# Inverse-transform steps ahead of spectra, and four attention scores in a row behind the last maxima, in a long convolution beside attention

## The chip, the cores and the metric

The kernel runs on one core of a Trainium2 chip. TensorE (PE) does the matmuls, VectorE (DVE), ScalarE (ACT) and GpSimd (POOL) the elementwise work, and nearly all transfers are issued from the queue of SyncE (SP). Each of these executes its own instruction stream in order, and the streams meet at semaphores. The metric is the device time of one launch in microseconds (us); the time before is the median of three runs.

## The reference

Two independent halves are computed from one sequence of 2048 rows and written side by side into one output of 2 x 448 columns.

```python
def _A_ref(u, log_A_real, A_imag, C_real, C_imag, log_dt, D_skip):
    dt = jnp.exp(log_dt)
    A = -jnp.exp(log_A_real) + 1j * A_imag
    C = (C_real + 1j * C_imag) * dt[:, None]
    P = jnp.exp((A * dt[:, None])[:, :, None] * pos[None, None, :])
    K = 2.0 * jnp.einsum("dn,dnl->dl", C, P).real        # D=448, N=256, L=2048
    Kf = jnp.fft.rfft(K, 2 * L)
    Uf = jnp.fft.rfft(u_t, 2 * L)
    y = jnp.fft.irfft(Uf * Kf[None], 2 * L)[:, :, :L]
    return y.transpose(0, 2, 1) + u * D_skip

def _B_ref(x, wqkv, wo):                                 # S=2048, D=448, H=16, Dh=28
    q, k, v = ...                                        # x @ wqkv, by head
    p = softmax(einsum("bhqd,bhkd->bhqk", q, k) * Dh ** -0.5)
    o = einsum("bhqk,bhkd->bhqd", p, v)
    return o.transpose(0, 2, 1, 3).reshape(B, S, D) @ wo
```

The first half is a convolution as long as the sequence, done with a transform, a product of spectra and an inverse transform. The second half is softmax attention without a mask, with 16 heads of width 28.

## The kernel before

A first stage projects x to queries, keys and values and prepares tables for the convolution's kernel. The second stage, the main loop (L1073 on), is the larger part. It has 256 steps, numbered s here. A step is one key tile of 128 keys (kt, 0 to 15) for one unit u; a unit is four heads (a group) and 512 queries, so 16 units make 4 groups by 4 query chunks. In each step TensorE computes four scores of 128 keys by 512 queries (`s0` to `s3`, tiles `pss`, function `s_mm`), ScalarE takes their exponentials (tiles `p`), and TensorE multiplies the exponentials of the step before with the values (`pv`, tile `po`; four matmuls that each use 32 columns of the array). The maxima of the softmax are computed 19 steps ahead by a second set of score matmuls (`m0` to `m3`, tiles `pm`, read by VectorE and ScalarE). With s = 237 the last maxima are done, and the remaining 19 steps, 237 to 255, have no `m`.

The convolution and the output projection are fed into the same loop through slots. One call of `slot` does at most one task. A step has two slots, A ahead of `pv` and B behind it, and from s = 238 a third, C, at the step's end (`FX`). The order of a step is the tuple `ORDER`: m0 s0 m1 s1, slot A, pv, slot B, m2 s2 m3 s3. Everything is emitted in program order, and the engines keep that order. The tasks that a slot can take in the last part are these:

- A **spectrum** (16 of them, 8 for each half of the channels; function `spectrum`): two forward tasks (`yk` with `mw`, 16 matmuls of 32 columns each in the profile's rows), whose results VectorE multiplies with the transformed input (`pr`), then four joins on GpSimd (`p`, function `join`), then two inverse tasks `back` (`p` with `mw`), which ScalarE evicts (`y`) and SP writes to DRAM (`z`). Between the second forward task and the first `back` lie at least GAP = 3 slots. The first two joins give the first `back` its operand, the last two the second.
- A **finish** (8 of them, 4 for each half; function `finish`), the last inverse step: its load brings `zi` from `z` and the input rows `ut`; GpSimd multiplies `ut` with D_skip (the skip); then four tasks of 8 matmuls each (`zi` with `wb`) are added to the skip by VectorE (`ot`) and written out, two at a time. A half's finishes can only be loaded when its eight spectra are done, since `zi` reads what they wrote. The first task of a finish comes three steps after its load at the earliest, and the load of the next one is issued when the first task of this one is placed.
- A **projection** of the attention output (four per query chunk in the last group; 32 matmuls `ua` with `og` and `on`), due when a unit is finished and its divisions by the softmax sums are done on VectorE (`divide`: `rb`, `r`, `pm`, then `on` or `og`). `load_og` loads the three earlier groups' outputs of that chunk at kt = 9 and places their divisions 3, 6 and 9 slots later, each with its second part two slots behind.

When nothing more urgent is due, a slot tries a spectrum first and then a finish, `f_slot(s_, "s") or f_slot(s_, "f")`. Behind the last step the same function empties what is left, two slots to a unit of s.

PSUM has eight banks. In the last part three of them hold `pss`, one `po`, and four are a ring from which all other matmul results are taken in turn (`w_tile`, names `pm`): a task has to wait until the result that was put into its bank four takings earlier has been read.

Of the kernel before, what the change touches and what calls it, by code (L numbers as in the profile page):

```python
# [8 lines left out]
F32 = mybir.dt.float32  # L9
# [13 lines left out]
G = 4  # L23
HG = H // G
CQ = 512
NQ = L // CQ
NK = L // 128
# [5 lines left out]
NS = NU * NK  # L33
LEAD = 3
ORDER = ('m0', 's0', 'm1', 's1', 'v', 'f', 'pv', 'f', 'v', 'k', 'm2', 's2', 'm3', 's3', 'v')
PB = 8
F1 = 2
FX, PD, GAP = 1, 2, 3
# [54 lines left out]
def body(ctx, tc, a, out):  # L93
# [5 lines left out]
    def pool(stack, name, bufs=1, space=None, side=None):  # L99
        kw = {} if space is None else {"space": space}  # L100
        if side:
            kw["side"] = side
        return stack.enter_context(tc.tile_pool(name=name, bufs=bufs, reuse_waits="tile", **kw))
# [23 lines left out]
    def w_tile():  # L127

        n_ring[0] += 1
        return ps_w[0].tile([128, CQ], F32, name=f"pm{n_ring[0] % ps_w[1]}")  # L130
# [25 lines left out]
    def load_v(g, c):  # L156
        v_g[g, c] = t = v_p.tile([128, NK // NQ, HG, 32], F32, name="v", bufs=5)
        nc.sync.dma_start(t.rearrange("p t h e -> p t (h e)"), v_d[c][:, g])

    def load_kd(g, j, rows=range(4)):  # L160
        if 0 in rows:
            kd_g[g, j] = kd_p.tile([128, CQ], F32R, name=f"kdif{j}")
        t = kd_g[g, j]
        for r in rows:
            nc.sync.dma_start(t[r::4].bitcast(F32), kd_d[g][r % 2, 32 * j:32 * j + 32, :])
# [62 lines left out]
    with ExitStack() as st:  # L228
# [368 lines left out]
        for i in range(16):  # L597
            for kc in range(4):
                f, kw = (max_mm, (0, i, kc)) if kc < 2 else (max_pair, (i, kc))
# [13 lines left out]
    ps_s = pool(att, "ps_s", 3, PSUM)  # L613
# [153 lines left out]
            wo_t.append(t)  # L767

    def s_mm(u, kt, j):
        pss = ps_s.tile([128, CQ], F32, name="pss")  # L770
        nc.tensor.matmul(pss, kt_g[u // NQ][j][:, kt * 128:(kt + 1) * 128], q_u[u][:, j, :], start=True, stop=True)
        p = kq_p.tile([128, CQ], F32, name="p", bufs=PB)
        nc.scalar.activation(p, pss, AF.Exp, scale=SCALE)
        return p
# [10 lines left out]
    def divide(o, y, at, then=lambda: None):  # L785

        t_ = {}

        def sums():
            t = kq_p.tile([128, NK, 32], F32, name="rb")  # L790
            nc.vector.transpose(t.rearrange("p b e -> p (b e)"), o)
            t_["r"] = kq_p.tile([128, NK], F32, name="r", bufs=2)
            nc.vector.reciprocal(t_["r"], t[:, :, DH])

        def scale():
            pw = w_tile()
            nc.vector.transpose(pw.rearrange("p (b e) -> p b e", e=32), t_["r"][:, :, None].to_broadcast([128, NK, 32]))
            nc.vector.tensor_tensor(y, o, pw, ALU.mult)
            then()
        later(at, sums)  # L800
        later(at + 2, scale)

    def load_og(u):
        og_u[u] = og = kq_p.tile([128, G - 1, CQ], F32, name="og")
        for g in range(G - 1):
            nc.sync.dma_start(og[:, g], on_d[u % NQ][g])
            divide(og[:, g], og[:, g], n_slot[0] + 3 + 3 * g, lambda: ready.append(u))

    def fin(u, s_):
        g, c = divmod(u, NQ)  # L810
# [122 lines left out]
    urgent, free, ready = collections.deque(), [], []  # L933

    def later(at, f):
        free.append((at, f))
        free.sort(key=lambda t: t[0])
# [9 lines left out]
    def u_part(i, c):  # L947
        u_jobs[i][1 + c]()
        if c and i not in (14, 15):
            u_load(i + 2)  # L950
        if c and i == 15:
            u_load(16)
            u_load(17)
        if c and i == 31:
            load_wo()
# [12 lines left out]
    n_slot, f_next = [0], {"s": 0, "f": 0}  # L968
# [6 lines left out]
    def f_load(s_, kind):  # L975

        if not f_jobs[kind] or f_loaded[kind]:
            return
        _, f, i = f_jobs[kind][0]
        if kind == "f" and s_done[0] < (f + 1) * N1 // 4:  # L980
            return
        if (kind, f, i) == ("f", 0, 0):
            if f_ready["s", 1] == NS:
                return
            f_p["f", 0] = f_p["f", 1] = pool(f1_st, "ff_p")
        if (kind, f) not in f_p or f_ready.get((kind, f), 0) > s_ + 2:
            return
        load, tasks, ahead = job(f_jobs[kind].popleft(), f_p[kind, f], kq_p, w_tile)
        load()
        if ahead:  # L990
            f_ahead.append((s_ + FL[kind] - 1, ahead))
        f_loaded[kind].append((max(f_ready.get((kind, f), 0), s_ + FL[kind]), tasks))

    def f_slot(s_, kind):
        f_load(s_, kind)
        if k_due or powers["e"] or powers["g"]:
            return False
        while f_ahead and f_ahead[0][0] <= s_:
            f_ahead.popleft()[1]()
        if not f_tasks[kind]:  # L1000
            if not f_loaded[kind] or f_loaded[kind][0][0] > s_:
                return False
            f_tasks[kind].extend(f_loaded[kind].popleft()[1])
            f_load(s_, kind)
        gap, t = f_tasks[kind][0]
        if n_slot[0] < f_next[kind] + gap:
            return False
        f_tasks[kind].popleft()
        t()
        s_done[0] += kind == "s" and not f_tasks[kind]  # L1010
        f_next[kind] = n_slot[0]
        f_load(s_, kind)
        return True
# [10 lines left out]
    def slot(s_):  # L1024
        n_slot[0] += 1
        while free and free[0][0] <= n_slot[0]:
            free.pop(0)[1]()
        if urgent and urgent[0][0] <= n_slot[0]:
            urgent.popleft()[2]()
        elif s_ >= NS and f_slot(s_, "s"):  # L1030
            pass
        elif p_due and p_due[0][0] <= s_:
            p_due.popleft()[1]()
        elif m_due and m_due[0][0] <= s_:
            m_due.popleft()[1]()
        elif u_due and u_due[0][0] <= s_:
            u_part(*u_due.popleft()[1:])
        else:
            f_slot(s_, "s") or f_slot(s_, "f")

    def k_seed(s_):
        b = k_due[0] if k_due else NB
# [32 lines left out]
    for s in range(NS):  # L1075
        u, kt = divmod(s, NK)
        sm = s + NK + LEAD
        if s == 12 * NK:
            k0_st.close()
            f_p["s", 0] = f_p["s", 1] = pool(f0_st, "f0_p", side="right")  # L1080
            f_ready["s", 0], f_ready["s", 1] = s, NS
        if s >= 12 * NK and f_ready["s", 1] == NS and not (k_due or m_due or powers["g"] or powers["e"]):
            g_st.close()
            ps_st.close()
            ps_w[:] = pool(ps_st, "ps_f", 4, PSUM), 1
            f_ready["s", 1] = s + F1
        if kt == 9 and u // NQ == G - 1:
            load_og(u)
        late[0] = s + NK + LEAD > NS
        if u % NQ == NQ - 1 and u < NU - 1 and kt % 4 == 2:  # L1090
            load_v(u // NQ + 1, kt // 4)
        if sm < NS and sm // NK % NQ == NQ - 1 and sm % NK % 4 == 0 and sm % NK and sm // (NQ * NK) + 1 < G:
            load_kd(sm // (NQ * NK) + 1, sm % NK // 4 - 1)
        if sm < NS and sm % (NQ * NK) == 0 and sm:
            load_kd(sm // (NQ * NK), HG - 1)
        if kt % 4 == 1 and u % NQ == 1 and u // NQ + 1 < G:
            load_k(u // NQ + 1, kt // 4, k_pools[(u // NQ + 1) % 2])
        if kt == 2:
            if u + 2 < NU:
                load_q(u + 2)  # L1100
        ps = []
        for op in ORDER:
            if op[0] == "s":
                ps.append(s_mm(u, kt, int(op[1])))
            elif op[0] == "f":
                slot(s)
            elif op[0] == "v":
                vec()
            elif op == "k":
                k_next()  # L1110
                k_begin(s)
                k_seed(s)
                for _ in range(3):
                    if powers["e"]:
                        powers["e"].popleft()()
            elif op == "pv":
                if prev:
                    pv_step(*prev)
                    if prev[1] == NK - 1:
                        fin(prev[0], s)  # L1120
            elif sm < NS:
                max_mm(sm // NK, sm % NK, int(op[1]))
        for _ in range(FX if late[0] else 0):
            slot(s)
        if sm < NS and sm % NK == NK - 1:
            def end(un=sm // NK):
                max_end(un, w_tile())
                max_put(un)
            max_join(sm // NK)
            soon_slot(UG[0], end)  # L1130
        k_next()
        prev = (u, kt, ps)
    pv_step(*prev)
    fin(prev[0], NS)
    s = NS
# [62 lines left out]
```

## Time and profile before

| | us |
|---|---|
| median of three runs | 1262.38 (1261.55 to 1264.51) |
| the profiled execution | 1263.07 |
| its span in the profile | 1261.3 |
| first score of the steps without maxima (s = 237) | about 1153.7 |
| last `back` of a spectrum starts | 1205.86 |
| last `pv` ends, ScalarE evicts the last `o` | 1241.95 |

The span is the time from the first to the last recorded instruction. Each slice of the profile's picture of 40 equal slices is 31.5 us wide, so the steps without maxima and what follows are the last three and a half slices. A busy TensorE is not TensorE at its peak, since the ends of matmuls are modelled. So what matters is the start times of its instructions, their distance from each other, and the idle time that a row shows in square brackets with its releaser.

### The profile page before, as it was taken

How to read it: one execution, taken by the hardware profiler on the slowest of the kernel's cores; microseconds unless marked ns; L12 is line 12 of the kernel's file. 1: busy time of each engine (PE TensorE's matmuls, PEld its weight loads, DVE VectorE, ACT ScalarE, POOL GpSimd, SP SyncE). 2: the span in 40 equal slices, each digit the busy share in tenths (PEclk: the TensorE clock that was granted, in tenths of full speed). 3: DMA queues.
4: the chain of work that ended last, by engine and by line, in shares of the span. 5: the costliest groups of instructions: out<-in, count | busy, mean ns of one | idle time of the engine just before them, and what ended most of it. 6: DMA issues, size and time to landing. Idle time of an engine off the chain costs nothing.

```text
span 1261.3 us, 31227 instructions
## 1 busy us (share of the span) xinstructions
PE 1195.8 (95%) x11569; PEld 671.1 (53%) x11569; DVE 944.0 (75%) x2138; ACT 957.7 (76%) x2146; POOL 843.2 (67%) x728
## 2 busy tenths in 40 slices
PE   6788888999999999999999999999999999999998
PEld 4666664455555555555555555555555545444333
DVE  5788966777877787878788988888887856756232
ACT  5878865688888888888878888888887656656453
POOL 2656750798788888878699999999994222333321
PEclk8999899899999999999999999999999999999999
DMA  6678889437664635475533133522314534557675
GB/s 198 216 259 286 284 276 350 141 86 186 173 155 110 176 116 162 125 237 169 178 97 105 50 89 93 161 84 71 105 38 148 190 134 162 188 174 219 209 200 134
DMA packets 203504, 206.08 MB, mean 163 GB/s; under 512 B 98328, under 2 KB 162392, under 8 KB 201304
## 3 DMA queue, kind: packets, MB, share of 16 engines
q1 hardware_dynamic: 202824, 203.50, 53.1%
q8 instruction: 91, 1.49, 0.5%
q10 hardware_dynamic: 528, 0.59, 0.2%
q14 instruction: 61, 0.50, 0.1%
HBM read 121.59 MB, written 82.18 MB: 162 GB/s over the span
## 4 chain that ended last, share of the span: by engine, by line
PE 77%; DVE 10%; ACT 4%; POOL 3%; issue 3%; DMA 3%; ACTq 0%; SPq 0%; POOLq 0%; DVEq 0%
PE pm L77 43%; PE pss L77 17%; PE po L77 16%; DVE tri L77 2%; DVE mx L77 1%; ACT rl L77 1%; DMA ut<-in_A_u 1%; ACT tri L77 1%; DVE sg L77 1%; DVE hl L77 1%; DVE px L77 1%; POOL qhat L77 1%; POOL p L77 1%; DMA zi<-z 1%; PE pt L77 1%
## 5 line engine op out<-in xcount | busy, mean ns | idle before, releaser
L77 ACT ACTIVATE p<-pss 128x512 f32<-128x512 f32 x1024 | 561.2, 611 | 122.1 <-PE pss L77 118.7
L77 PE MATMUL pss<-qhat,khat 128*128 128x512 f32 x1024 | 402.3, 399 | 1.7 <-ACT p L77 1.7
L77 DVE TENSOR_REDUCE mx<-pm 128x1 f32<-128x512 f32 x480 | 308.1, 683 | 90.4 <-PE pm L77 89.1
L77 PE MATMUL pm<-khat,qhat 128*128 128x512 f32 x749 | 326.6, 439 | 8.2 <-ACT rl L77 5.2
L77 PE MATMUL po<-p,v 128*32 128x512 f32 x2048 | 268.7, 594 | 0.0
L77 POOL TENSOR_TENSOR e<-e,sdb 128x256 f32<-128x256 f32 x168 | 201.8, 1201 | 99.0 <-ACT e L77 50.1
L77 PEld LDWEIGHTS pm<-khat,qhat 128*128 128x128 f32 x749 | 141.1, 189 | 221.7 <-ACT p L77 63.7
L77 POOL TENSOR_TENSOR e<-e,eu 128x256 f32<-128x256 f32 x168 | 248.1, 1477 | 13.2
L77 DVE CUSTOM_DVE_ANT_0 rl<-pm,rl 128x512 f32<-128x512 f32 x259 | 178.2, 688 | 67.3 <-ACT rl L77 64.5
L77 PEld LDWEIGHTS pss<-qhat,khat 128*128 128x128 f32 x1024 | 190.8, 189 | 45.3 <-issue 10.6
L77 POOL TENSOR_TENSOR eu<-e,sdb 128x256 f32<-128x256 f32 x168 | 201.9, 1202 | 0.0
L77 POOL TENSOR_TENSOR p<-pr,pr 64x448 f32<-64x448 f32 x64 | 73.1, 1142 | 143.4 <-PE pm L77 72.1
L77 ACT ACTIVATE rl<-pm 128x512 f32<-128x512 f32 x259 | 156.7, 606 | 15.4 <-PE pm L77 9.3
L77 DVE TENSOR_TENSOR g<-g,zg 128x128 f32<-128x128 f32 x392 | 162.4, 414 | 3.7
L77 PE MATMUL pm<-kdif,qhat 128*128 128x512 f32 x249 | 100.2, 402 | 6.4 <-DVE xn L77 4.3
L77 PE MATMUL pm<-xh,khat 128*128 128x512 f32 x256 | 84.3, 421 | 11.8 <-DVE hl L77 5.0
L77 DVE TENSOR_TENSOR zg<-g,zg 128x128 f32<-128x128 f32 x224 | 88.2, 394 | 5.5
L77 PEld LDWEIGHTS pm<-e,g 128*32 128x32 f32 x3584 | 55.6, 110 | 39.9 <-issue 12.7
L77 DVE TENSOR_TENSOR pr<-pm,ub 128x448 f32<-128x448 f32 x64 | 36.7, 616 | 52.1 <-PE pm L77 43.2
L77 PE MATMUL pm<-e,g 128*32 128x64 f32 x3584 | 73.3, 222 | 2.0 <-POOL e L77 1.3
L77 ACT ACTIVATE y<-pm 128x448 f32<-128x448 f32 x48 | 26.5, 553 | 58.5 <-PE pm L77 36.9
L77 PEld LDWEIGHTS po<-p,v 128*32 128x32 f32 x2048 | 54.9, 110 | 25.8 <-issue 20.8
(134 smaller groups left out, 1390.9 us busy)
## 6 DMA issues: line engine op xcount, KB each, us to landing
sdb<-sd SPq DMA_DIRECT2D x55, 336.0 KB
qhat<-q SPq DMA_DIRECT2D x64, 256.0 KB
khat<-k SPq DMA_DIRECT2D x64, 256.0 KB
sd<-sg SPq DMA_DIRECT2D x8, 1456.0 KB
k<-hl SPq DMA_DIRECT2D x16, 512.0 KB
mw<-in_mw SPq DMA_DIRECT2D x16, 512.0 KB
sd<-qhat SPq DMA_DIRECT2D x8, 896.0 KB
yu_d<-ub SPq DMA_DIRECT2D x64, 112.0 KB
```

What stands on the lines that cost most here:

```text
L77: i = f(*args, **kw)
```

## The change

Five edits are made. (1) Where a slot chose a spectrum first and a finish second, it now chooses a finish first. (2) The special rule that behind the last step spectra go ahead of everything else is gone. (3) In the steps without maxima the four scores stand in a row at the step's start (`ORDER_END`). (4) From s = 237 the fourth score takes its bank from the ring of four (`w_tile`) instead of from the three banks of `pss`. (5) `load_og` is called at kt = 8 instead of 9, and its divisions come 6, 9 and 12 slots later instead of 3, 6 and 9.

```diff
@@ constants
 ORDER = ('m0', 's0', 'm1', 's1', 'v', 'f', 'pv', 'f', 'v', 'k', 'm2', 's2', 'm3', 's3', 'v')
+ORDER_END = ('s0', 's1', 's2', 's3', 'v', 'f', 'pv', 'f', 'v', 'k', 'v')
@@ s_mm
-        pss = ps_s.tile([128, CQ], F32, name="pss")
+        pss = w_tile() if j == HG - 1 and u * NK + kt + NK + LEAD >= NS else ps_s.tile([128, CQ], F32, name="pss")
@@ load_og
-            divide(og[:, g], og[:, g], n_slot[0] + 3 + 3 * g, lambda: ready.append(u))
+            divide(og[:, g], og[:, g], n_slot[0] + 6 + 3 * g, lambda: ready.append(u))
@@ slot
         if urgent and urgent[0][0] <= n_slot[0]:
             urgent.popleft()[2]()
-        elif s_ >= NS and f_slot(s_, "s"):
-            pass
         elif p_due and p_due[0][0] <= s_:
...
         else:
-            f_slot(s_, "s") or f_slot(s_, "f")
+            f_slot(s_, "f") or f_slot(s_, "s")
@@ main loop
-        if kt == 9 and u // NQ == G - 1:
+        if kt == 8 and u // NQ == G - 1:
             load_og(u)
...
-        for op in ORDER:
+        for op in ORDER if sm < NS else ORDER_END:
```

The instruction streams of the two kernels are the same up to s = 226. From there they differ in order. In steps 226 to 236 the slots of before hold seven `back` tasks, six forward tasks and five finish tasks; those of after hold one `back` task, two forward tasks and fourteen finish tasks. All sixteen finish tasks of the first half are done by s = 238 in the changed kernel, and six spectra are left for s = 239 to 251 where before had three.

The first place is TensorE's stream around one of the last spectra. In before, from slot C of s = 239 to slot B of s = 241, `yk` with `mw` is a forward task and `p_...` with `mw` a `back` task of the same spectrum:

```order
L77 MATMUL pm_16952<-yk_16809,mw 32x224 x8
L77 MATMUL pss<-qhat,khat 128x512 x2
L77 MATMUL pm_16973<-yk_16809,mw 32x224 x8
L77 MATMUL po<-p,v 32x512 x4
L77 MATMUL pm_16999<-zi,wb 32x224 x4
L77 MATMUL pss<-qhat,khat 128x512 x2
L77 MATMUL pm_17025<-zi,wb 32x224 x4
L77 MATMUL pss<-qhat,khat 128x512 x2
L77 MATMUL pm_17040<-p_16986,mw 32x224 x8
L77 MATMUL po<-p,v 32x512 x4
L77 MATMUL pm_17060<-p_16989,mw 32x224 x8
```

In the changed kernel, from slot C of s = 247 to slot B of s = 249 (`pm_...` from `qhat` and `khat` is the fourth score):

```order
L78 MATMUL pm_17337<-yk_17230,mw 32x224 x8
L78 MATMUL pss<-qhat,khat 128x512 x3
L78 MATMUL pm_17366<-qhat,khat 128x512
L78 MATMUL pm_17370<-yk_17230,mw 32x224 x8
L78 MATMUL po<-p,v 32x512 x4
L78 MATMUL pss<-qhat,khat 128x512 x3
L78 MATMUL pm_17405<-qhat,khat 128x512
L78 MATMUL pm_17410<-p_17383,mw 32x224 x8
L78 MATMUL po<-p,v 32x512 x4
L78 MATMUL pm_17426<-p_17386,mw 32x224 x8
```

The four scores of a step have become one run, and between the second forward task and the first `back` two finish tasks are gone: `pv` and the scores are all that is left there.

The second place is TensorE's last steps. In the changed kernel the last `back` stands in slot B of s = 251, and s = 252 and 253 have no task. From the scores of s = 254 on:

```order
L78 MATMUL pss<-qhat,khat 128x512 x3
L78 MATMUL pm_17612<-qhat,khat 128x512
L78 MATMUL pm_17622<-zi,wb 32x224 x4
L78 MATMUL po<-p,v 32x512 x4
L78 MATMUL pm_17632<-zi,wb 32x224 x4
L78 MATMUL pm_17640<-zi,wb 32x224 x4
L78 MATMUL pss<-qhat,khat 128x512 x3
L78 MATMUL pm_17658<-qhat,khat 128x512
L78 MATMUL pm_17662<-zi,wb 32x224 x4
L78 MATMUL po<-p,v 32x512 x8
L78 MATMUL pm_17692<-zi,wb 32x224 x4
L78 MATMUL pm_17701<-zi,wb 32x224 x4
```

The first `zi` here is the first task of the second half's first finish. Behind these rows follow four projections with a finish task behind each of the first three, and then seven more finish tasks. So twelve finish tasks stand behind the last `pv` (the second four of `po` x8); before had five there, one ahead of the four projections and one behind each of them.

The third place is the end of SP's queue. Before, from the third finish of the second half:

```order
L77 DMA zi<-z_99 128x8x224
L77 DMA ut<-in_A_u 64x4x224 x2
L77 DMA out<-ot 64x2x224 x4
L77 DMA zi<-z_99 128x8x224
L77 DMA ut<-in_A_u 64x4x224 x2
L77 DMA out<-ot 64x2x224 x4
L77 DMA out<-y 128x448 x2
L77 DMA out<-ot 64x2x224 x2
L77 DMA out<-y 128x448 x2
L77 DMA out<-ot 64x2x224 x2
```

In the changed kernel, likewise from the third finish:

```order
L78 DMA zi<-z_99 128x8x224
L78 DMA ut<-in_A_u 64x4x224 x2
L78 DMA out<-ot 64x2x224 x2
L78 DMA out<-y 128x448 x2
L78 DMA out<-ot 64x2x224 x2
L78 DMA out<-y 128x448
L78 DMA zi<-z_99 128x8x224
L78 DMA ut<-in_A_u 64x4x224 x2
L78 DMA out<-y 128x448
L78 DMA out<-ot 64x2x224 x8
```

The last finish's load (`zi`, `ut`) has moved behind three of the four rows of projected output (`out<-y`), and eight output rows of finishes (`out<-ot`) follow it instead of two to four.

## The prediction

> **What bounds the kernel now.** I read the page's chain first, then busy time by windows, then the time line of TensorE's own queue, and last the time line of all engines around the places that move.
>
> ```profile
> PE 77%; DVE 10%; ACT 4%; POOL 3%; issue 3%; DMA 3%; ACTq 0%; SPq 0%; POOLq 0%; DVEq 0%
> ```
>
> TensorE carries 77% of the chain. The streams differ only from s = 226 on, the last 165 us, and there the windows show that it is not always TensorE:
>
> ```profile
> 1220.00:1240.00 20.00, 17.26 (x132) 6.76 (x136) 9.98 (x22) 12.13 (x24) 4.37 (x3) 1.00 0.89 221
> 1240.00:1262.00 22.00, 16.04 (x184) 6.82 (x176) 4.63 (x10) 3.59 (x7) 2.08 (x1) 0.96 0.43 114
> ```
>
> The columns are window, width, busy time of PE, PEld, DVE, ACT and POOL, clock, DMA share, GB/s. TensorE lacks about 3 us in the first window and 6 in the second, at a clock of 0.96 to 1.00. So latencies between engines already matter here, and I price the change by following TensorE's new row of work and the latencies that it meets.
>
> **Steps 226 to 236, with maxima.** TensorE's rows, each the first max score behind slot B:
>
> ```profile
> 1107.72 0.50 PE L77 MATMUL pm<-khat,qhat 128*128 128x512 f32 x1
> 1114.60 0.50 PE L77 MATMUL pm<-khat,qhat 128*128 128x512 f32 x1
> 1121.05 0.50 PE L77 MATMUL pm<-khat,qhat 128*128 128x512 f32 x1
> ...
> 1130.15 0.50 PE L77 MATMUL pm<-khat,qhat 128*128 128x512 f32 x1
> 1133.98 0.50 PE L77 MATMUL pm<-khat,qhat 128*128 128x512 f32 x1
> 1136.03 0.96 PE L77 MATMUL pm<-p,mw 128*32 128x224 f32 x16
> 1138.54 0.50 PE L77 MATMUL pm<-khat,qhat 128*128 128x512 f32 x1
> ```
>
> A step with a projection and one spectrum task takes 6.88 us (1107.72 to 1114.60), with a finish task instead 6.45. A step with two finish tasks takes 3.83 (1130.15 to 1133.98), with two spectrum tasks 4.56. The change swaps spectrum for finish tasks in three steps of the first kind (3 x 0.43 = 1.3) and five of the second (5 x 0.73 = 3.65), and one step goes the other way (0.73). One more is even: a single forward task against two finishes. So the changed kernel reaches s = 237 4.2 us earlier. The loads of the first half's finishes are issued as early as before or earlier.
>
> **Steps 237 to 251, the last six spectra.** Durations on TensorE, and the latency of the joins (all engines' rows):
>
> ```profile
> 1167.47 0.74 PE L77 MATMUL pss<-qhat,khat 128*128 128x512 f32 x2
> 1168.14 0.96 PE L77 MATMUL pm<-yk,mw 128*32 128x224 f32 x16
> 1168.92 1.04 PE L77 MATMUL po<-p,v 128*32 128x512 f32 x8
> 1169.78 0.56 PE L77 MATMUL pm<-zi,wb 128*32 128x224 f32 x8
> 1170.78 4.75 POOL L77 TENSOR_TENSOR p<-pr,pr 64x448 f32<-64x448 f32 x4 [5.82 <-PE pss L77]
> 1173.16 0.96 PE L77 MATMUL pm<-p,mw 128*32 128x224 f32 x16 [0.97 <-POOL p L77]
> 1175.58 0.96 PE L77 MATMUL pm<-p,mw 128*32 128x224 f32 x16 [0.61 <-POOL p L77]
> 1178.69 2.46 PE L77 MATMUL pm<-ua,og 128*32 128x448 f32 x24
> 1181.73 1.04 PE L77 MATMUL po<-p,v 128*32 128x512 f32 x8
> 1182.58 0.94 PE L77 MATMUL pm<-yk,mw 128*32 128x224 f32 x16
> 1184.89 4.77 POOL L77 TENSOR_TENSOR p<-pr,pr 64x448 f32<-64x448 f32 x4 [3.00 <-DVE pr L77]
> ```
>
> From start to start a spectrum task costs 0.78 us ahead of `pv` or of another task (1168.14 to 1168.92), and I take 0.88 ahead of scores, because there the array changes over as it does behind a finish task (0.49 instead of 0.4). `pv` costs 0.86, a projection 3.04 (1178.69 to 1181.73). A pair of scores between two tasks costs 0.67 and eight in a row 2.05 (1133.98 to 1136.03), so one more score costs 0.23 and four in a row 1.13. Edit (3) is worth 2 x 0.67 - 1.13 = 0.21 us in a step whose slot C is filled, at most 4 us over 19 steps, and less where a step waits anyway. In steps with empty slots edit (4) takes away the wait of the fourth score for ScalarE:
>
> ```profile
> 1214.58 0.97 PE L77 MATMUL pss<-qhat,khat 128*128 128x512 f32 x3
> 1215.83 0.49 PE L77 MATMUL pss<-qhat,khat 128*128 128x512 f32 x1 [0.28 <-ACT p L77]
> ```
>
> That is 0.28 us in each of two steps. The new bank is free in time, since what was put there four takings earlier belongs to the step before; I price its wait at nothing until s = 255.
>
> Against this stand the joins. From the start of the second forward task F to the end of the second join lie 1184.89 + 2.39 - 1182.58 = 4.7 us, and 7.1 to the end of the fourth (5.0 and 7.4 in the first example). Before covered part of this with two finish tasks or a projection and still waited (0.97 and 0.61). Now little lies there but `pv` and one run of scores. With t = 0 at the first score of s = 237:
>
> - s = 237, 238 and 239 up to the first F: (0.9 + 0.4 + 0.86 + 0.25) + (1.13 + 0.4 + 0.86 + 0.78 + 0.88) + (1.13 + 0.78 + 0.86) = 9.2. The 0.25 is the transpose that ends the last maxima, an estimate below the finish task's 0.4.
> - To the second F: last `back` at F + 7.1, then 0.88 + 1.13 + 0.78 + 0.86, so 10.8. TensorE has work for 3.7 of the 7.1.
> - To the third, with two projections: 7.1 + 0.88 + 1.13 + 3.04 + 0.86 + 0.78 = 13.8. The cover holds but for 0.4.
> - To the fourth, with two projections: all TensorE: 2 x (1.13 + 3.04 + 0.86) + 3 x 0.88 + 0.78 + 1.13 = 14.6.
> - To the fifth and the sixth: 7.1 + 0.78 + 0.88 + 1.13 = 9.9 each, and 7.1 to the last `back`. TensorE has work for 4.4 of each 7.1.
>
> The last `back` starts at t = 75.3. About 12 us of this is TensorE waiting for joins (3.4 + 0.4 + 3 x 2.7). Each spectrum's loads are issued some 8 us ahead of their use; I price them at nothing, and if that cover is too short, the next forward task starts late.
>
> **Steps 252 to 255.** The second half's finishes can load only now. The chain in before, all engines:
>
> ```profile
> 1153.32 1.17 PE L77 MATMUL pss<-qhat,khat 128*128 128x512 f32 x3
> ...
> 1205.86 0.96 PE L77 MATMUL pm<-p,mw 128*32 128x224 f32 x16
> 1205.95 1.94 SPq L77 DMA_DIRECT2D z<-y  x2
> ...
> 1209.98 0.47 SPq L77 DMA_DIRECT2D zi<-z  x1
> 1210.50 2.16 SPq L77 DMA_DIRECT2D ut<-in_A_u  x2
> ...
> 1216.90 0.59 PE L77 MATMUL pm<-zi,wb 128*32 128x224 f32 x8 [0.58 <-DMA zi<-z]
> 1218.06 2.10 POOL L77 TENSOR_TENSOR ut<-ut,dsk 128x896 f32<-128x896 f32 x1 [13.27 <-DMA ut<-in_A_u]
> ```
>
> `zi` is issued 4.1 us after the last `back` starts, its first matmul runs 6.9 us after that, and the skip ends 10.2 us after it. So `zi` is issued at 79.4 and lands at 86.3. TensorE arrives at slot A of s = 254 at 75.3 + 0.88 + 2 x (1.13 + 0.86) + 1.13 = 81.3 and waits 5.0 us, with both last `pv` and the last scores behind it. The skip ends at 89.6. The first finish result leaves its bank only then (0.33 for `ot`, below), and the finish task of s = 255 needs that bank: 90.0. Add 0.4, two `pv` and 0.6 until the last result stands; ScalarE evicts `o` at 92.7. Before did so at 1241.95 - 1153.7 = 88.3: the three scores at 1153.32 are the last of s = 236 and the first two of s = 237, so t = 0 of before is about 1153.7 and `o` stands in the next rows.
>
> **Behind the last step.**
>
> ```profile
> 1232.83 0.98 DVE L77 TENSOR_TENSOR ot<-pm,ut 128x224 f32<-128x224 f32 x3
> ...
> 1235.97 0.55 SPq L77 DMA_DIRECT2D zi<-z  x1
> ...
> 1241.95 0.60 ACT L77 ACTIVATE o<-po 128x512 f32<-128x512 f32 x1 [1.14 <-PE po L77]
> ...
> 1243.92 2.08 POOL L77 TENSOR_TENSOR ut<-ut,dsk 128x896 f32<-128x896 f32 x1 [6.33 <-DMA ut<-in_A_u]
> ...
> 1253.58 3.72 SPq L77 DMA_DIRECT2D out<-y  x2
> ...
> 1256.72 0.39 DVE L77 TENSOR_TENSOR ot<-pm,ut 128x224 f32<-128x224 f32 x1 [2.99 <-PE pm L77]
> 1257.39 1.25 SPq L77 DMA_DIRECT2D out<-ot  x2
> ```
>
> In before the third output row of projections is issued 11.6 us after `o` (1253.58), and the span ends 2.7 us behind the last issue (1261.3 against 1258.64). In the changed queue the last finish's load stands behind that third row: 92.7 + 11.6 + 0.4 = 104.7. From the issue of `zi` to the end of its skip lie 10.0 us (1235.97 to 1246.00): 114.7. Two `ot` at 0.33 to 115.4, 0.3 to the issue (1257.39 against the end of the `ot` ahead of it), two pairs of output rows at 1.25, 2.7 to the end: t = 120.8. Before needed 1261.3 - 1153.7 = 107.6.
>
> Edits (2) and (5) I price at nothing: no spectrum is left behind s = 255, and the last unit's divisions are done by s = 252, while VectorE idles for the joins. If the `og` rows came late, `on` and the projections would be late by as much.
>
> **The sum.** 120.8 - 107.6 - 4.2 = +9.0 us: steps 237 to 255 take 4.4 us longer, and what follows 8.8. The profiled execution took 1263.07 us, 1.8 outside its span and 0.7 above the median, so I put the difference on the median: 1262.4 + 9.0 = 1271.4. Each of the two exposed loads is bounded by 5.5 us below (B) and 11 above (D); I take the 8 of the nearest rows.
>
> **The rivals.** (B) The exposed loads are shorter, because little else moves then. For it speaks the best window of the end:
>
> ```profile
> 1158.00:1160.00 2.00, 2.00 (x33) 0.81 (x28) 1.62 (x3) 0.85 (x2) 1.91 (x1) 1.00 1.03 408
> ```
>
> `zi` and both `ut` are 1376 KB, 3.4 us at 408 GB/s. With 2.1 us for the way (z's issue ended at 1207.89, `zi` followed at 1209.98) a load takes 5.5 us instead of 8.1, and two of them save 5.2: +3.8, 1266.2. Against it, the last load before (1235.97 to 1243.92) took 8.0 beside only four output rows. [...]
>
> (C) Not slower: the joins cost no wait, because VectorE and GpSimd, freed of skips and finishes, deliver earlier. It needs the fourth join within 3.7 to 4.4 us of F instead of 7.1. Then some 12 us vanish: -3.0, 1259.4. Against it, four joins alone take 4.75.
>
> (D) Later still: the second finish's load, now issued right behind the first's, shares its engines with it, as two in before:
>
> ```profile
> 1217.97 0.37 SPq L77 DMA_DIRECT2D zi<-z  x1
> 1229.02 2.11 POOL L77 TENSOR_TENSOR ut<-ut,dsk 128x896 f32<-128x896 f32 x1 [8.86 <-DMA ut<-in_A_u]
> ```
>
> That is 11.0 us instead of 8.1, and with one spectrum's load late by 1 us it is +4 more, 1275.4.
>
> **How the numbers follow.** My forecast has a chance of 0.64, B 0.14, C 0.10, D 0.12. About 0.2%, 2.5 us, is what a measurement can tell from no change. Faster gets 0.06 of C and 0.02 of B's low end, the same 0.04 of C and 0.06 from B and the low end of my own, slower the rest, 0.82. The range, 1263.5 to 1278, takes in B and D with some 2.6 us about each, the size of the dispute on one load, and leaves out C.
>
> **What would show it.** The first score of s = 237 some 4 us earlier; TensorE rows released by `p` of GpSimd in four of the last six spectra, with the last `back` some 75 us behind that score; a `zi` wait of about 5 us ahead of the last two steps; the last `ut` skip as the last wait of the chain, some 10 us behind its issue. The prediction is wrong if the finish tasks of the first half wait for their loads, if the joins hide, or if the last load is not behind the third projected row.

## The result, and the profile after

The changed kernel takes 1273.28 us (median of four runs, 1272.99 to 1276.03), the kernel before, run four times, 1261.97. The ratio is 1.0087, with a 95% interval of 1.0068 to 1.0105: about 11 us slower. The profiled execution has a span of 1271.4 us against 1261.3.

Where the 10.1 us of the two spans lie is told by three places. The rows of before, from the time line: the load of the earlier groups' outputs for the last unit, and the first projection of s = 226, which I call the entry of the last part.

```profile
1056.28 1.43 SPq L77 DMA_DIRECT2D og<-on  x3
...
1095.91 2.46 PE L77 MATMUL pm<-ua,og 128*32 128x448 f32 x24
```

The same places in the changed kernel:

```profile
1049.38 1.63 SPq L78 DMA_DIRECT2D og<-on  x3
...
1096.83 2.46 PE L78 MATMUL pm<-ua,og 128*32 128x448 f32 x24
```

The first row of each corrects a sentence of the description above: TensorE's tasks are the same up to s = 226, but edit (5) moves loads and divisions of the units before already, so that the streams of SP and VectorE differ earlier. The changed kernel reaches the entry 0.9 us later. Then come TensorE's rows around the six spectra and behind them:

```profile
1149.42 1.68 PE L78 MATMUL pss<-qhat,khat 128*128 128x512 f32 x4
1150.94 0.40 PE L78 MATMUL pm<-qhat,khat 128*128 128x512 f32 x1
...
1159.44 0.94 PE L78 MATMUL pm<-yk,mw 128*32 128x224 f32 x16
1160.31 0.97 PE L78 MATMUL pss<-qhat,khat 128*128 128x512 f32 x3
1161.11 0.39 PE L78 MATMUL pm<-qhat,khat 128*128 128x512 f32 x1
1161.43 1.06 PE L78 MATMUL po<-p,v 128*32 128x512 f32 x8
1164.15 0.96 PE L78 MATMUL pm<-p,mw 128*32 128x224 f32 x16 [1.65 <-POOL p L78]
1166.56 0.96 PE L78 MATMUL pm<-p,mw 128*32 128x224 f32 x16 [1.45 <-POOL p L78]
...
1170.23 0.94 PE L78 MATMUL pm<-yk,mw 128*32 128x224 f32 x16
1178.22 0.96 PE L78 MATMUL pm<-p,mw 128*32 128x224 f32 x16 [1.16 <-POOL p L78]
...
1219.28 0.96 PE L78 MATMUL pm<-yk,mw 128*32 128x224 f32 x16
1224.01 0.96 PE L78 MATMUL pm<-p,mw 128*32 128x224 f32 x16 [1.77 <-POOL p L78]
1226.43 0.96 PE L78 MATMUL pm<-p,mw 128*32 128x224 f32 x16 [0.60 <-POOL p L78]
1235.90 0.59 PE L78 MATMUL pm<-zi,wb 128*32 128x224 f32 x8 [3.14 <-DMA zi<-z]
...
1261.35 1.72 PE L78 MATMUL pm<-zi,wb 128*32 128x224 f32 x32 [2.32 <-DMA zi<-z]
```

The first row holds the last score of s = 236 and the first three of s = 237, so t = 0 is at about 1149.8. From the entry to it are 53.0 us; before needed 57.8 (1095.91 to 1153.7). So steps 226 to 236 gave 4.8 us. The reader then sees what TensorE waits for: after the second forward task (`yk`) of four of the six spectra only `pv` and one run of scores stand ready, and the `back` tasks (`p` with `mw`) wait for GpSimd's joins, 1.65 and 1.45 us at the first spectrum, 1.77 and 0.60 at the last. One of the other two, which have projections there, waits 1.16 us (1178.22), the other not at all. In all, such waits take 11.4 us here, against 2.9 in before.

Busy time by windows. The columns are those of the prediction. First the total of before from s = 237 to the end:

```profile
sum 107.60, PE 95.55 PEld 38.64 DVE 33.81 ACT 50.52 POOL 30.76; mean PE 31.85 PEld 12.88 DVE 11.27 ACT 16.84 POOL 10.25
```

Then three windows of the changed kernel and their total:

```profile
1150.00:1228.00 78.00, 66.55 (x744) 30.45 (x744) 28.65 (x53) 41.22 (x82) 30.84 (x28) 1.00 0.48 160
1228.00:1244.00 16.00, 12.86 (x107) 6.30 (x109) 1.42 (x5) 8.78 (x18) 3.63 (x2) 0.89 0.78 202
1244.00:1271.40 27.40, 16.27 (x209) 6.90 (x200) 6.54 (x16) 2.18 (x4) 4.73 (x3) 0.93 0.71 193
sum 121.40, PE 95.68 PEld 43.65 DVE 36.62 ACT 52.17 POOL 39.21; mean PE 31.89 PEld 14.55 DVE 12.21 ACT 17.39 POOL 13.07
```

TensorE is busy for nearly the same time in both, 95.6 and 95.7 us, in 107.6 us before and 121.4 after (the windows begin 0.2 us behind t = 0). The tasks are not the same: spectrum tasks have moved in here and finish tasks out, and a part of the busy time after is spent at a lower clock (0.89 in the second window). The loss of this stretch, 14.0 us from t = 0, shows as idle TensorE. It splits at the eviction of the last `o`: 5.2 us up to it (93.5 against 88.3) and 8.7 behind it (28.1 against 19.4). 0.9 - 4.8 + 5.2 + 8.7 are the 10 us.

The chain that ended last carries 74% of TensorE instead of 77. These are pieces of it (start, us, what):

```profile
1228.08 2.05 DMA z<-y
...
1230.28 5.48 DMA zi<-z
...
1243.32 0.61 ACT o L78
...
1256.82 6.38 DMA ut<-in_A_u
```

SP's queue shows why the last of them starts so late:

```profile
1255.19 0.34 SPq L78 DMA_DIRECT2D out<-y  x1
1255.62 0.39 SPq L78 DMA_DIRECT2D zi<-z  x1
1256.10 1.35 SPq L78 DMA_DIRECT2D ut<-in_A_u  x2
```

The load of the last finish stands behind the third projected row, which SP can issue only when that row exists, 11.9 us after `o`. GpSimd's rows:

```profile
1173.43 4.73 POOL L78 TENSOR_TENSOR p<-pr,pr 64x448 f32<-64x448 f32 x4 [6.92 <-DVE pr L78]
...
1201.78 4.73 POOL L78 TENSOR_TENSOR p<-pr,pr 64x448 f32<-64x448 f32 x4 [9.42 <-PE pss L78]
...
1237.83 2.09 POOL L78 TENSOR_TENSOR ut<-ut,dsk 128x896 f32<-128x896 f32 x1 [11.45 <-DMA ut<-in_A_u]
...
1263.36 2.07 POOL L78 TENSOR_TENSOR ut<-ut,dsk 128x896 f32<-128x896 f32 x1 [9.32 <-DMA ut<-in_A_u]
```

Four joins take 4.73 us, about as before. The first and the last skip of the second half start 7.6 and 7.7 us after their `zi` was issued, and end 9.6 and 9.8 us after it.

### The profile page after: what moved, and what is told of

It reads as the page before. It is cut to its first block, busy times and chain, and to the rows that moved or that the text cites. A ratio compares the mean times of both kernels' runs of the same rounds, so it can differ in the third digit from the quotient of the medians.

```text
span 1271.4 us, 31222 instructions
## 1 busy us (share of the span) xinstructions
PE 1191.9 (94%) x11569; PEld 672.4 (53%) x11569; DVE 944.8 (74%) x2138; ACT 957.4 (75%) x2146; POOL 843.9 (66%) x728
## 4 chain that ended last, share of the span: by engine, by line
PE 74%; DVE 11%; POOL 4%; ACT 4%; issue 3%; DMA 2%; ACTq 0%; SPq 0%; POOLq 0%; DVEq 0%
PE pm L78 41%; PE pss L78 16%; PE po L78 16%; DVE tri L78 2%; POOL p L78 1%; ACT rl L78 1%; POOL qhat L78 1%; DVE mx L78 1%; ACT tri L78 1%; DVE sg L78 1%; DVE px L78 1%; ACT p L78 1%; DVE rl L78 1%; DVE hl L78 1%; DVE qhat L78 1%
## 5 line engine op out<-in xcount | busy, mean ns | idle before, releaser
L78 ACT ACTIVATE p<-pss 128x512 f32<-128x512 f32 x1005 | 550.2, 610 | 119.4 <-PE pss L78 116.7
L78 PE MATMUL pss<-qhat,khat 128*128 128x512 f32 x1005 | 392.9, 397 | 0.1
L78 PEld LDWEIGHTS pss<-qhat,khat 128*128 128x128 f32 x1005 | 188.2, 189 | 37.3 <-ACT p L78 5.8
L78 PEld LDWEIGHTS pm<-e,g 128*32 128x32 f32 x3584 | 55.6, 109 | 40.0 <-issue 12.3
L78 ACT ACTIVATE y<-pm 128x448 f32<-128x448 f32 x48 | 26.4, 551 | 64.3 <-PE pm L78 36.5
```

Of the source, the lines that this page charges most:

```text
L78: i = f(*args, **kw)
```

## The experiments

The theory was the prediction's: edit (1) alone makes the loss, because it uses up the finish tasks that covered the spectra's joins and leaves the second half's finishes bare at the end; edits (3) and (4) gain a little, (2) and (5) nothing. Edit (2) has no kernel of its own. Its rule acts only behind the last step, and in every kernel here the last `back` lies more than 10 us ahead of the last `o` (1226.43 and 1243.32 in the changed one), so it finds no spectrum to put first. Four kernels take the change apart, four price single waits, and two follow something that the trace showed. "Entry" and "rest" are of the one profiled execution of each: the entry as above, and the span from there to its end.

| kernel | median us (lowest to highest, runs) | ratio to before (95%) | entry | rest |
|---|---|---|---|---|
| before | 1261.97 (1261.35 to 1264.51, 4) | | 1095.91 | 165.4 |
| the change | 1273.28 (1272.99 to 1276.03, 4) | 1.0087 (1.0068 to 1.0105) | 1096.83 | 174.6 |
| edits 3, 4 alone | 1259.82 (1256.59 to 1261.74, 11) | 0.9977 (0.9968 to 0.9986) | 1096.92 | 161.7 |
| edits 1, 2 alone | 1275.22 (1272.50 to 1277.17, 4) | 1.0097 (1.0081 to 1.0112) | 1094.64 | 176.1 |
| edit 5 alone | 1263.07 (1260.46 to 1265.13, 11) | 1.0005 (0.9996 to 1.0014) | 1096.37 | 164.1 |
| all but edit 1 | 1258.57 (1256.68 to 1260.23, 6) | 0.9964 (0.9952 to 0.9976) | 1096.19 | 160.8 |
| the change, half joins | 1265.02 (1263.49 to 1265.73, 10) | 1.0019 (1.0010 to 1.0028) | 1098.00 | 165.9 |
| the change, no second skips | 1268.07 (1267.72 to 1268.57, 4) | 1.0045 (1.0031 to 1.0060) | 1096.53 | 170.1 |
| the change, rows from ScalarE | 1272.08 (1271.69 to 1272.54, 4) | 1.0077 (1.0064 to 1.0090) | 1097.80 | 172.9 |
| all but edit 1, rows from ScalarE | 1259.84 (1256.09 to 1262.70, 12) | 0.9976 (0.9966 to 0.9987) | 1096.96 | 160.8 |
| the change, busy wait | 1273.82 (1273.29 to 1274.22, 4) | 1.0088 (1.0075 to 1.0101) | 1097.59 | 174.8 |
| all but edit 1, busy wait | 1259.37 (1257.82 to 1262.76, 12) | 0.9976 (0.9967 to 0.9986) | 1098.26 | 161.8 |

Before was run again beside the experiments and gave 1262.56, 1262.54 and 1262.65 in the three sets (the first four kernels, the next four, the last two).

**Edits 3 and 4 alone: the run of four scores.**

```diff
+ORDER_END = ('s0', 's1', 's2', 's3', 'v', 'f', 'pv', 'f', 'v', 'k', 'v')
...
-        pss = ps_s.tile([128, CQ], F32, name="pss")
+        pss = w_tile() if j == HG - 1 and u * NK + kt + NK + LEAD >= NS else ps_s.tile([128, CQ], F32, name="pss")
...
-        for op in ORDER:
+        for op in ORDER if sm < NS else ORDER_END:
```

> The kernel before with edits (3) and (4) alone: four scores in a row from s = 237, the fourth from the ring of four. Theory (the change loses by its order of tasks, not by these two edits): 0.21 us in each of some 12 steps whose slot C is filled and 0.28 us in each of the steps with empty slots, less what a waiting step absorbs, so 2 to 4 us faster than before, 1258 to 1260. Rival (the fourth score's bank in the ring holds up the tasks of the slots): not faster, or up to 4 us slower.

It is 2.7 us faster by the medians. A run of four scores costs 1.12 us in the changed kernel (1160.31 to 1161.43, above), where two pairs cost 2 x 0.67 in before, and the waits of 0.28 us for ScalarE are gone.

**Edits 1 and 2 alone: finish ahead of spectrum.**

```diff
-        elif s_ >= NS and f_slot(s_, "s"):
-            pass
...
-            f_slot(s_, "s") or f_slot(s_, "f")
+            f_slot(s_, "f") or f_slot(s_, "s")
```

> The kernel before with edits (1) and (2) alone: a slot chooses a finish ahead of a spectrum. Theory (the spectra lose their cover and the second half's finishes are pushed to the end): slower than before by 9 to 13 us, somewhat more than the whole change, since the saving of the score run is missing. Rival (the loss of the whole change comes from the fourth score's bank or from the moved divisions): within 3 us of before.

It is 12.7 us slower, by the medians 1.4 more than the whole change, though the intervals of the two ratios overlap. TensorE's rows, around the first and the last spectrum behind the maxima and ahead of the first `zi` of the second half:

```profile
1162.63 0.96 PE L77 MATMUL pm<-p,mw 128*32 128x224 f32 x16 [1.05 <-POOL p L77]
1165.05 0.96 PE L77 MATMUL pm<-p,mw 128*32 128x224 f32 x16 [0.79 <-POOL p L77]
...
1223.27 0.96 PE L77 MATMUL pm<-p,mw 128*32 128x224 f32 x16 [1.23 <-POOL p L77]
1225.68 0.96 PE L77 MATMUL pm<-p,mw 128*32 128x224 f32 x16 [0.59 <-POOL p L77]
1227.84 0.50 PE L77 MATMUL pss<-qhat,khat 128*128 128x512 f32 x1 [0.30 <-ACT p L77]
...
1234.84 0.59 PE L77 MATMUL pm<-zi,wb 128*32 128x224 f32 x8 [1.08 <-DMA zi<-z]
```

The joins are waited for at the first and at the last three of the six spectra, and for less long (7.4 us in all instead of 11.4): TensorE is held longer by other things there, by two pairs of scores instead of a run of four and by waits for ScalarE of the kind that the last row but one shows and that edit (4) takes away.

**Edit 5 alone.**

```diff
-            divide(og[:, g], og[:, g], n_slot[0] + 3 + 3 * g, lambda: ready.append(u))
+            divide(og[:, g], og[:, g], n_slot[0] + 6 + 3 * g, lambda: ready.append(u))
...
-        if kt == 9 and u // NQ == G - 1:
+        if kt == 8 and u // NQ == G - 1:
```

> The kernel before with edit (5) alone: the earlier groups' outputs loaded one step earlier, their divisions placed 6, 9 and 12 slots later. Theory: within 1.5 us of before. Rival (it explains why the changed kernel reached s = 226 0.9 us later than before): slower by about 1 us, with the same 0.9 us at s = 226.

The interval holds 1: no difference can be told. It reaches up to 1.0014, 1.8 us, so that the rival's 1 us is not ruled out by the time, and the entry of one execution, 1096.37, does not decide it either. With 12.7 - 2.7 + 0.5 = 10.5 the medians of the parts add up to nearly the 11 of the whole.

**All but edit 1.** The changed kernel with the spectra tried first again.

```diff
-            f_slot(s_, "f") or f_slot(s_, "s")
+            f_slot(s_, "s") or f_slot(s_, "f")
```

> The changed kernel with edit (1) undone: spectra first, finishes second, the rest as changed. Theory: all of the loss goes, and the score run's saving stays, so 1258 to 1261, 12 to 15 us faster than the changed kernel. Rival (edits 3 to 5 carry a part of the loss): above 1264.

It is 4.0 us faster than before and 14.7 faster than the changed kernel, and has the lowest median of all versions, below both kernels. The `back` tasks that wait, and the first `zi` of the second half:

```profile
1162.42 0.96 PE L78 MATMUL pm<-p,mw 128*32 128x224 f32 x16 [1.02 <-POOL p L78]
1164.83 0.96 PE L78 MATMUL pm<-p,mw 128*32 128x224 f32 x16 [0.59 <-POOL p L78]
...
1172.64 0.96 PE L78 MATMUL pm<-p,mw 128*32 128x224 f32 x16 [1.32 <-POOL p L78]
1175.06 0.96 PE L78 MATMUL pm<-p,mw 128*32 128x224 f32 x16 [0.60 <-POOL p L78]
...
1214.79 0.59 PE L78 MATMUL pm<-zi,wb 128*32 128x224 f32 x8 [1.90 <-DMA zi<-z]
```

Two spectra wait, for 3.5 us in all, instead of five for 11.4, and the second half's first `zi` is used 21 us earlier. That edit (1) is the cause is shown from both sides: with nothing beside it but edit (2), which finds no spectrum to act on, the whole loss is there, and without it the loss is gone. Whether this kernel is faster than edits 3 and 4 alone can't be told; the intervals overlap.

**The joins' price: half joins.** Each join computes the first half of its elements only, and both halves of the `back` task read those.

```diff
-            nc.gpsimd.tensor_tensor(t_["p", e][:64], t_[0, 0][es], t_[1, 1][es], ALU.subtract)
-            nc.gpsimd.tensor_tensor(t_["p", e][64:], t_[0, 1][es], t_[1, 0][es], ALU.add)
+            nc.gpsimd.tensor_tensor(t_["p", e][:64, :1], t_[0, 0][es][:, :1], t_[1, 1][es][:, :1], ALU.subtract)
+            nc.gpsimd.tensor_tensor(t_["p", e][64:, :1], t_[0, 1][es][:, :1], t_[1, 0][es][:, :1], ALU.add)
...
-                mm32(pf[:, m, :DF], t_["mw"][:, 2 * m + e, 128:], t_["p", e][:, m, :], start=True, stop=True)
+                mm32(pf[:, m, :DF], t_["mw"][:, 2 * m + e, 128:], t_["p", e][:, 0, :], start=True, stop=True)
```

> The changed kernel with the joins on GpSimd cut to half their columns (64x224 instead of 64x448; the second half of each inverse operand is taken from the first, so half of the joins is left out). Theory (four of the last six spectra wait for the fourth join, 7.1 us behind the second forward task): that join ends at about 4.7 instead of 7.1, TensorE's own work there is 3.7 to 4.4, so some 2 to 2.4 us less for each of these four or five spectra, the last inverse task 8 to 11 us earlier behind s = 237 and the whole 7 to 11 us faster than the changed kernel, 1262 to 1266. Rival (the spectra wait for VectorE's products or for their loads, and the joins only come last): less than 3 us.

It is 8.3 us faster than the changed kernel by the medians, 8.7 by the rest. The last four joins on GpSimd take 2.83 us instead of 4.74, less than half off:

```profile
1215.97 2.83 POOL L78 TENSOR_TENSOR p<-pr,pr 64x224 f32<-64x224 f32 x4 [5.35 <-PE pss L78]
```

The only wait that these four leave on TensorE, and the first `zi` of the second half:

```profile
1217.40 0.96 PE L78 MATMUL pm<-p,mw 128*32 128x224 f32 x16 [0.83 <-POOL p L78]
1228.26 0.98 PE L78 MATMUL pm<-zi,wb 128*32 128x224 f32 x8 [2.89 <-DMA zi<-z]
```

The waits for joins fall from 11.4 to 3.7 us, by 7.7, and the time by about as much; from the entry to the last `back` it is 8.6 us less (121.0 against 129.6). So this waiting lies on the path that sets the end, and rival C, in which the joins are hidden, is out.

**The skips' price: no second skips.** The second half's input rows are neither loaded nor multiplied nor added; its finish results are copied out as they are.

```diff
-            t_["u"] = p.tile([128, 4, DF], F32, name="ut", bufs=2)
-            for m in range(2):
+            if f == 0:
+                t_["u"] = p.tile([128, 4, DF], F32, name="ut", bufs=2)
+            for m in range(2 if f == 0 else 0):
...
+            if f == 0:
                 nc.vector.tensor_tensor(jbi(ot[:, i], "p (j b i)"), jbi(pf, "p (b j i)"), jbi(t_["u"][:, i], "p (j b i)"), ALU.add)
+            else:
+                nc.vector.tensor_copy(jbi(ot[:, i], "p (j b i)"), jbi(pf, "p (b j i)"))
...
-        return load, [(0, lambda i=i: one(i)) for i in range(4)], skip
+        return load, [(0, lambda i=i: one(i)) for i in range(4)], skip if f == 0 else None
```

> The changed kernel without the skip in the second half's finishes (neither the input rows are loaded nor multiplied nor added there; VectorE copies the result instead). Theory (the last load's skip is the last wait, and the first one's holds a ring bank at s = 255): about 2 to 3 us at s = 255 and 3.5 us at the end, so 5 to 7 us faster than the changed kernel, 1266 to 1268. Rival (the loads of z bind by themselves, or the output rows do): less than 2 us.

It is 5.2 us faster than the changed kernel by the medians, 4.5 by the rest. Nearly all of that lies behind the last `o` (23.9 us, from 1242.66 on, instead of 28.1); up to `o` only 0.4 is gained. So the last skip and its load are on the path with some 4 us, the first with next to nothing: there the load of `zi` and a low clock (below) hold TensorE nearly as long.

**The queue's price: rows from ScalarE.** The projected rows are issued from ScalarE's queue, so that the last finish's load no longer stands behind the third of them.

```diff
-            nc.sync.dma_start(out[q0:q0 + 128, D:], y)
+            nc.scalar.dma_start(out[q0:q0 + 128, D:], y)
```

> The changed kernel with the projected output rows issued from ScalarE's queue, so that the last finish's load no longer stands behind the third of them on SP. Theory: the load leaves when the second finish's output rows are issued, some 1.9 us earlier, and the kernel is 1.5 to 2.5 us faster than the changed one. Rival (the load's own bank or the shared transfer engines set its landing): no difference.

By the medians it is 1.2 us faster than the changed kernel, below the 1.5 that I had given as the least. The load in its SP queue:

```profile
1254.69 0.55 SPq L78 DMA_DIRECT2D zi<-z  x1
1255.33 1.33 SPq L78 DMA_DIRECT2D ut<-in_A_u  x2
```

It leaves 10.4 us after `o` (1244.33) instead of 12.3, and from `o` to the end are 26.4 us instead of 28.1; 1.7 by the rest. The mechanism is as told and worth 1.7 us in the profile, and the medians, taken in two different sets of runs, show less of it.

**The same edit in the best version** (all but edit 1).

> Edits (2) to (5) with spectra first, and the projected output rows issued from ScalarE's queue. No load stands behind these rows there. Theory: 0 to 0.5 us faster than without the move, 1258 to 1259, through the last output rows alone. Rival (the issues hold up ScalarE's evictions): slower than without the move.

1259.84 against 1258.57, with the same rest of 160.8 us: no gain; whether it is slower can't be told, since the intervals overlap. In the version with SP's rows the last load is issued at 1232.91, ahead of `o` (1237.74), and its skip runs from 1240.71 on, ahead of the first projected row at 1242.51. So no load stood behind a row there.

**The clock behind a wait.** In the changed kernel the windows behind the wait for `zi` show something that the prediction had not reckoned with. The last column but two is the granted clock of TensorE:

```profile
1236.00:1237.00 1.00, 1.00 (x16) 0.64 (x19) 0.00 (x0) 0.00 (x0) 0.00 (x0) 0.84 1.16 227
1237.00:1238.00 1.00, 1.00 (x10) 0.33 (x5) 0.00 (x0) 0.00 (x0) 0.17 (x1) 0.50 1.10 310
...
1239.00:1240.00 1.00, 1.00 (x6) 0.62 (x3) 0.05 (x1) 0.00 (x0) 0.92 (x1) 0.50 1.14 307
```

For over 3 us the granted clock is at half: `pv` takes 1.59 us there instead of 1.04 to 1.07, two finish tasks 1.80 instead of 0.94 to 0.97. Two kernels keep TensorE busy in such a wait by computing a fourth score several times into the same bank.

```diff
-        nc.tensor.matmul(pss, kt_g[u // NQ][j][:, kt * 128:(kt + 1) * 128], q_u[u][:, j, :], start=True, stop=True)
+        for _ in range(1 + 12 * (j == HG - 1 and u * NK + kt == 254)):
+            nc.tensor.matmul(pss, kt_g[u // NQ][j][:, kt * 128:(kt + 1) * 128], q_u[u][:, j, :], start=True, stop=True)
```

> The changed kernel, with the fourth score of s = 254 computed thirteen times into the same bank instead of once (twelve more matmuls, some 2.7 us by 0.225 each), so that TensorE is busy through most of its 3.1 us of waiting for zi. Nothing is computed differently. Theory: the granted clock of 0.59 in the 4 us behind that wait comes from TensorE's idle time. Then the wait shrinks to some 0.4 us, the clock stays at 1.00, pv x8 takes about 1.05 instead of 1.59 and two finish tasks about 0.95 instead of 1.80. The finish task of s = 255 needs the bank that is free about 0.4 us before the place at which TensorE now arrives, so at most some 0.5 us are gained up to the last o, and the time falls by 0 to 0.8 us. Rival 1: the low clock comes from the transfers that run then (DMA share 1.1); it stays at about 0.6 and the time is the same. Rival 2: the 1.6 us of half clock are fully on the path; the time falls by 1.5 us or more.

TensorE's rows around the wait in this kernel:

```profile
1233.08 3.15 PE L78 MATMUL pm<-qhat,khat 128*128 128x512 f32 x13
1236.38 0.58 PE L78 MATMUL pm<-zi,wb 128*32 128x224 f32 x8 [0.15 <-DMA zi<-z]
1236.76 1.07 PE L78 MATMUL po<-p,v 128*32 128x512 f32 x8
...
1241.04 0.58 PE L78 MATMUL pm<-zi,wb 128*32 128x224 f32 x8 [1.34 <-DVE ot L78]
```

The clock stays at 1.00 and `pv` takes 1.07, although as much is transferred as in the changed kernel (a DMA share of 1.12 from 1236 to 1240 in both). So the half clock comes from TensorE's idle time and not from the transfers. The kernel without second skips says the same from the other side: there the clock was 0.58 from 1235 to 1239 at a DMA share of 0.55, against 0.59 at 1.12 in the changed kernel from 1236 to 1240. But the time is the same (1273.82, ratio 1.0088 with an interval of 1.0075 to 1.0101): the finish task of s = 255 now waits 1.34 us for the bank that the first finish result occupies until its skip is done. That is the wait that the prediction had put there; in the changed kernel the half clock takes up the time in its place.

For the best version, with six more matmuls at s = 249 in a wait of 1.90 us, behind which the clock fell to 0.66 on the mean of 4 us:

> The changed kernel with spectra first again (edit 1 undone), and with the fourth score of s = 249 computed seven times (six more matmuls, some 1.35 us), in the 1.9 us in which TensorE waits for the first zi of the second half. Nothing is computed differently. Theory: the wait shrinks to some 0.5 us, and the clock behind it stays at 1.00 instead of 0.66. What is gained there, up to 1.6 us, goes into the two waits that follow (0.85 us for ot, 0.86 us for og), which hang on loads and not on TensorE, so that the time falls by 0 to 0.8 us against the same kernel without the added matmuls (1258.57). Rival: the waits that follow move along, and the time falls by 1.5 us.

The wait shrinks to 1.01 us, the clock is 1.00, and the time is 1259.37 against 1258.57, not faster. Further on TensorE waits 1.21 us for the second finish's `zi`, where there was no wait without the added matmuls, and then for this:

```profile
1231.65 0.49 PE L78 MATMUL pm<-qhat,khat 128*128 128x512 f32 x1 [1.74 <-DVE ot L78]
```

This wait, for a bank that a finish result holds, was 0.85 us without the added matmuls. So the time won at the full clock went into the waits behind it here too.

## Why the prediction was right, point by point

The forecast was 1271.4 us and +9.0; the profiled spans differ by 10.1, the medians by 11.3. Its working against the trace, with t from the first score of s = 237:

| step | predicted | measured |
|---|---|---|
| steps 226 to 236 | -4.2 | -4.8, after an entry that came 0.9 late |
| first F, then the distances to the other five | 9.2; 10.8, 13.8, 14.6, 9.9, 9.9 | 9.6; 10.8, 14.7, 14.5, 9.9, 9.9 |
| last `back` starts | t = 75.3 | 76.6 |
| waits for joins | about 12 | 11.4 |
| `zi` issued after the last `back` | 4.1 | 3.85 |
| first `zi` matmul after its issue; TensorE's wait | 6.9; 5.0 | 5.6; 3.1 |
| skip ends after the issue of `zi`, first; last | 10.2; 10.0 | 9.6; 9.8 |
| last `o` evicted | t = 92.7 | 93.5 |
| third projected row issued after `o` | 11.6 | 11.9 |
| end | t = 120.8 | 121.6 |

**Right.** The three terms have the sizes that the text gave: +4.4 up to `o` came as 5.2, +8.8 behind it as 8.7, and -4.2 as -4.8. Each of the mechanisms was then moved by itself: the joins (leaving out half of their work took 8.3 us away), the second half's skips and their loads (5.2), the last load's place behind the third row (1.7 in the profile), the bank that the first skip holds (1.34 us of waiting when nothing else is in the way). Edits (3) and (4) gave 2.7 us, below the bound of 4 for the first and 0.56 for the second; edit (5) nothing that can be told from no change, and edit (2) finds no spectrum to act on. Five of the six spectra waited for joins, as in the prediction's sum; its list of signs named four.

**Mis-sized.** The load of `zi` landed 1.3 us sooner than the nearest row had it, so that TensorE waited 3.1 us and not 5.0. The next step of the working is right in size partly by luck. It had the finish task of s = 255 wait for the bank of the first finish result, at t = 90.0; in the changed kernel this task starts at 91.0 without waiting, because the half clock, which the prediction did not have, held TensorE a little longer than the bank would have. Without the half clock the bank's wait is there (1.34 us, above) and the time is the same. The distance from the second F to the third was 0.9 too short: the joins of that spectrum began 3.2 us after F (1170.23 to 1173.43) and not 2.4 as the fourth's did (1199.42 to 1201.78), since a division on VectorE stood between its two pairs of products. "VectorE idles for the joins" was true of the other five.

**The rivals.** B, with a load of 5.5 us up to the end of `zi` and both `ut`, is out: from the issue of `zi` to the start of the skip the two took 7.6 and 7.7 us. `zi` alone took 5.5 the first time. The 8.1 of the nearest rows was closer. C is out by the half joins. D was right in that the second finish's load, issued right behind the first's, takes longer (its skip starts 10.3 us after its issue, 1232.14 to 1242.45); that shared engines are the reason is not shown. But nothing on the path waited for it, and no forward task started late for its load.

**Not foreseen.** The entry. It differs between executions by more than I had thought: 1095.91, 1096.92 and 1094.64 in before and the kernels with edits 3, 4 and with edits 1, 2, whose streams are all the same up to there. So 1 us of a difference between two single profiles says nothing, and the part of the measured 11.3 us beyond the 9.2 of the rest is not assigned to a cause.

## What to carry to other kernels

When a scheduler may choose between a task with a long latency behind it and one that is pure work, the pure work is the cover for the gaps: used up early, it won 4.8 us here and left TensorE's remaining 95.6 us of busy time to take 14 us more. Price such a reordering by writing down the bounding engine's new row of tasks, meeting each latency with what stands ready at that moment, and asking which loads become possible only when the last long task is done. Before filling a wait, look at what the engine would wait for next: of four repairs tried here without leaving work out, one brought 1 to 2 us and three brought nothing, in two of them because another wait stood right behind, in the third because no load stood behind a row any more.

## What the runs showed of the hardware

- TensorE's granted clock fell around the wait for the second half's first `zi`. On the mean of 4 us it was 0.59 in the changed kernel (1236 to 1240), 0.66 in all but edit 1 (1214 to 1218), 0.58 without second skips (1235 to 1239) and 0.62 with half joins (1228 to 1232); the waits were 3.14, 1.90, 2.72 and 2.89 us long. In the changed kernel it was 0.84, three times 0.50 and 0.95 in the five windows of 1 us from 1236 on, and 1.00 on either side. Taken as one stretch at 0.50 between times at 1.00, these windows, and in the others the means above with those of the 4 us that adjoin (0.92 behind, 0.99 behind, 0.96 ahead), give an estimated 3.4 us each time, beginning between 0.6 us ahead of TensorE's restart (half joins) and 0.8 us behind it (the changed kernel). It stayed at 1.00 when the wait was filled with matmuls that nobody needs (1232 to 1244 in the changed kernel with the busy wait, 1210 to 1226 in all but edit 1 with it).
- The length of a wait alone does not decide. Ahead of the last finish's tasks TensorE waited 2.33 us with half joins, and the 32 matmuls behind it took 2.20 us (clock 0.87 from 1252 to 1256, 0.50 from 1256 to 1260); it waited 2.32 in the changed kernel and 2.24 in the one with the busy wait, and the same 32 took 1.72 (clock 1.00 from 1260 to 1264 in the changed kernel). The waits for joins, up to 1.78 us in the changed kernel, left it at 1.00 too (1150 to 1228). What else decides stays open.
- The distance to the next start depends on what follows. A finish task takes 0.40 us ahead of `pv` (1132.23 to 1132.63 in before) and 0.49 ahead of scores (1133.49 to 1133.98); two in a row ahead of scores take 0.87 to 0.90 (1160.65 to 1161.52 with edits 3, 4 alone, 1237.61 to 1238.51 in the changed kernel with the busy wait), which is the sum of the two, as the prediction had it.
